# An unconditional fast arm, two more unsplit heads, a new spread of weight conversions, and first loads in three pieces

## The chip, the cores and the metric

One core of one Trainium2 chip runs the program. The metric is device time in microseconds of one execution; the median of several executions is compared. One more execution was taken with the hardware profiler; its trace counts time from the first instruction of the program (its span).

## The reference, cut to what matters

Inputs are float32 apart from the two counts. The weights of the two mixing blocks come as float64 and are converted on the chip.

```python
# attention: B, H, S, D = 2, 8, 768, 64; n_global, n_local = 8, 96
scores = (q @ k^T) / sqrt(D)
keep = (column < n_global) or (0 <= row - column < n_local)
dist = n_local where global and not local, else |row - column|
scores = where(keep, scores - 2**-(h + 1) * dist, -1e9)
a = softmax(scores);  x = a @ v, as (B, S, 512)
# first mixing block
theta = x @ w_theta
y = w_tok_r @ (x * cos(theta)) + w_tok_i @ (x * sin(theta))
u = x + y;  x = u + relu(u @ w_ch)
# second mixing block, d_ff = 1024
h = relu(x @ w_in);  c = convolution of 3 taps of h along the sequence
out = (h * sigmoid(c)) @ w_out
```

The counts n_global and n_local are read on the chip. With at most 8 global columns and 1 to 97 local ones a row of 128 queries needs only a band of keys.

## The kernel before, in words

There are two arms. `run_fast` computes the banded attention and then the mixing blocks; `run_general` computes full rows of scores for any counts, and the same mixing blocks. `begin` runs ahead of both: it issues the first loads, keeps TensorE occupied with four products of zeros (`idle`), reads the two counts (`words`, `nf`), makes the table of distances and masks (`table`), and makes `fi`, which is 1 if the counts fit the band. Then line 1023 loads `fi` from SBUF into a register of each engine, and the branch of line 1026 picks the arm. The general arm lies behind the fast one in every engine's program, so an engine that has finished the fast arm jumps over it.

In the fast arm one head is 768 queries in six tiles of 128, handled in three steps of two tiles. The loop variable `j` counts these steps, `i, tp = divmod(j, 3)`, with 16 heads `i`, so j runs to NJ = 48 and on until the pipeline is empty. In each step the order on every engine is written out by hand: scores of step j (TensorE, into PSUM), softmax of j-1 (VectorE adds the table and takes the row minimum, `L378`), exponentials of j-2 or so (ScalarE, `L387`), transposes, copies to SBUF, products with v, and after three steps the division by the row sums (`L296` to `L298`).

Scores are made in two ways. Heads in `WHOLE` (0 to 7) multiply float32 by float32 as loaded: one product per tile, which the trace shows as two instructions. Other heads are split: ScalarE makes a rounded copy of the scaled queries (`L306`), VectorE makes the remainder of queries (`L310`) and of keys (`L92`, `qk<-a`, 64x816), and each tile takes two products of rounded operands. The rounded keys of a split head come by a DMA of GpSimd that converts (`keys`), but for head 10 (`ROUND`), where ScalarE makes them. Whole heads come in pairs of one load of keys and two of queries (`pair`), into parts of `scratch` and of the output tile of the second batch.

Beside the heads the loop runs the weight conveyor (`Net.run(k)` takes k steps). A weight tile takes six steps, four of them one VectorE instruction each (`L104`, `L108`, `L112` on `wbit`, and the remainder, `L92`, `wt<-wbit`), two of them one ScalarE instruction each. Twelve tiles (72 steps) are done in the attention, the other 36 in `Mix.tail`. After every pair of heads the finished output is transposed (`X<-ident,xs`), and from head 11 on `theta_0` adds six products of `theta` to each step. When the heads are through, `theta1` and `Mix.tail` do the rest: token mixing, channel mixing, `ff_in` with its gate, and `ff_out`, which writes the result.

```python
        if i > 0 and i + 1 not in WHOLE:
            if tp == 0:
                att.split(i + 1, "A A" if i + 1 in ROUND else "  A")
...
        if 7 < j <= NJ:
            net.run((3, 2, 3)[tp] if i > 10 else 2 if i < 7 else 1)
```

Of the kernel before, what the change touches and what calls it, by code (L numbers as in the profile page):

```python
# [12 lines left out]
F32 = mybir.dt.float32  # L13
F32R = mybir.dt.float32r
I32 = mybir.dt.int32
AF = mybir.ActivationFunctionType
ALU = mybir.AluOpType
# [4 lines left out]
P = 128  # L22
# [17 lines left out]
TWO_PI = 2.0 * math.pi  # L40
TURN = 6.283185
TWO32 = float(2.0 ** 32)
WHOLE = range(8)
ROUND = (10,)
LAG_SM, LAG_EXP, LAG_T, LAG_EV, LAG_PV, LAG_N = 1, 2, 3, 4, 5, 6


# [179 lines left out]
class Attention:  # L227
# [21 lines left out]
    def load(self, i, whole=False):  # L249
        if whole or (i < NH and i not in WHOLE):  # L250
            b, h = divmod(i, H)
            src, st = self.net.io["qk"][b, :, h, :], self.st[i % 2]
            if whole or i in ROUND:
                self.nc.sync.dma_start(st, src)
            else:
                self.nc.sync.dma_start(st[:, 0:S], src[:, 0:S])
                self.nc.sync.dma_start(st[D:P, S:STAGE], src[D:P, S:STAGE])

    def keys(self, i):
        if i < NH and i not in WHOLE and i not in ROUND:  # L260
            b, h = divmod(i, H)
            self.nc.gpsimd.dma_start(self.K(i), self.net.io["qk"][b, :, h, S:STAGE])

# [202 lines left out]
class Mix:  # L466
# [237 lines left out]
    def tail(self, early):  # L704
# [151 lines left out]
            n.run(4)  # L856
        pipe.drain()
        n.finish(48)
        for b in range(2):
            for t in range(NT):  # L860
                halves = [slice(0, DM // 2), slice(DM // 2, DM)] if (b, t) == (1, NT - 1) else [slice(0, DM)]
                for c in halves:
                    self.ff_out(b, t, bank(), "V" if c.start or t % 2 == 0 else "A", c)


def run_fast(tc, net):
# [2 lines left out]
    att = FastAttention(net, xs)  # L869
    mix = Mix(net, xs)  # L870
    nc.scalar.activation(att.whole[3][0:D], net.head["half_pi"][0:D].to_broadcast([D, S]), AF.Copy, scale=0.0)
    att.tables(1)
    nc.gpsimd.memset(att.whole[2][D:P], 0.0)
    att.load_v(0)
    att.pair(2)
    att.load_v(1)
# [31 lines left out]
    for j in range(NJ + LAG_N + 3):  # L908
# [23 lines left out]
                att.keys(i + 2)  # L932
        if i > 0 and i + 1 not in WHOLE:
            if tp == 0:
                att.split(i + 1, "A A" if i + 1 in ROUND else "  A")
            elif tp == 1:
                att.split(i + 1, "   V")
                att.split(i + 1, " V")
# [26 lines left out]
            next(early, None)  # L965
        if j == 4:
            net.fetch()
        if 7 < j <= NJ:
            net.run((3, 2, 3)[tp] if i > 10 else 2 if i < 7 else 1)
    last.drain()  # L970
    mix.tail(early)


# [36 lines left out]
def arm(tc, io, head, run):  # L1010
    with tc.tile_pool(name="small", bufs=1) as small, tc.tile_pool(name="slots", bufs=1) as slots, tc.tile_pool(
        name="ps", bufs=1, space=bass.MemoryType.PSUM
    ) as ps, tc.manual_schedule():
        run(tc, Net(tc, io, small, slots, ps, head))


def build(nc, io):
    with tile.TileContext(nc) as tc, tc.tile_pool(name="const", bufs=1) as small:
        head = {}
        net = Net(tc, io, small, None, None, head)  # L1020
        with tc.tile_pool(name="idle", bufs=1, space=bass.MemoryType.PSUM) as ps, tc.manual_schedule():
            begin(nc, io, net, small, head, ps.tile([P, 512], F32, name="idle"))
        rv = nc.values_load(
            head["flag"][:1, :1], min_val=0, max_val=1, skip_runtime_bounds_check_because="it is the product of comparisons, 0 or 1"
        )
        with tc.If(rv == 1) as cmp:
            arm(tc, io, head, run_fast)
        with cmp.Else():
            arm(tc, io, head, run_general)


def begin(nc, io, net, small, head, idle):
# [1 line left out]
    w = small.tile([P, 4], I32, name="words")  # L1034
    scratch = small.tile([P, 2584], F32, name="scratch")
    nc.scalar.dma_start(w, io["n"].bitcast(I32).rearrange("(o n) -> o n", o=1).to_broadcast([P, 4]))
    for x in (slice(0, 2 * KW), slice(2 * KW, NT * KW)):
        nc.sync.dma_start(scratch[:, S:STAGE][:, x], io["pairs"][0, :, x])
    nc.sync.dma_start(scratch[D:P, STAGE : STAGE + S], io["qk"][0, D:P, 1, 0:S])
    qc = (slice(0, 2 * P), slice(2 * P, S))  # L1040
    for x in qc:
        nc.scalar.dma_start(scratch[0:D, x], io["qk"][0, 0:D, 0, x])
    nc.vector.memset(scratch[D:P, 0:S], 0.0)
    zero = nc.const_aps.tensor(0.0, [P, 512], F32)
    for x in (512, 512, 512, 128):
        net.mm(idle[:, 0:x], zero[:, 0:P], zero[:, 0:x], True, True)
    nc.vector.memset(scratch[0:D, STAGE : STAGE + S], 0.0)

# [18 lines left out]
    nc.vector.scalar_tensor_tensor(f[:, 4:6], lo2, 0.0, hi2, op0=ALU.is_lt, op1=ALU.add)  # L1067
    nc.vector.scalar_tensor_tensor(f[:, 6:8], f[:, 4:6], TWO32, lo2, op0=ALU.mult, op1=ALU.add)
    ng, nl = f[:, 6:7], f[:, 7:8]
    flag = small.tile([1, 2], F32, name="flag")  # L1070
    fi = small.tile([1, 1], I32, name="fi")
    nc.vector.tensor_scalar(flag[:, 0:1], nl[0:1], 1.0, None, op0=ALU.is_ge)
    nc.vector.scalar_tensor_tensor(flag[:, 1:2], nl[0:1], float(NPREV + 1), flag[:, 0:1], op0=ALU.is_le, op1=ALU.mult)
    nc.vector.scalar_tensor_tensor(fi, ng[0:1], float(NG), flag[:, 1:2], op0=ALU.is_le, op1=ALU.mult)
    far = small.tile([P, NG], F32, name="far")
    nc.gpsimd.tensor_scalar(far, R[:, G], ng, BIG, op0=ALU.is_ge, op1=ALU.mult)
    nc.gpsimd.tensor_scalar(far, far, nl, FIRST, op0=ALU.max, op1=ALU.mult)
# [3 lines left out]
    nc.vector.tensor_tensor(X[:, 0:NG], X[:, 0:NG], far, op=ALU.max)  # L1081
    nc.vector.tensor_copy(T[:, G], far)
    nnl = small.tile([P, 1], F32, name="nnl")
    head.update(scratch=scratch, qk0=qk0, table=table, ident=ident, half_pi=hp[:, 0:1], ng=ng, nl=nl, nnl=nnl, flag=fi)


# [34 lines left out]
```

## Time and profile before

| what | value |
| --- | --- |
| median of 3 runs | 409.94 us (407.86 to 410.41) |
| profiled execution, its own time | 407.4 us |
| its span, first to last instruction | 405.5 us |
| TensorE matmuls (PE) busy | 398.0 us, 98% |
| weight loads (PEld) busy | 375.5 us, 93% |
| VectorE (DVE) busy | 323.5 us, 80% |
| ScalarE (ACT) busy | 222.2 us, 55% |
| GpSimd (POOL) busy | 27.0 us, 7% |

The profiled execution's own time is 1.9 us longer than its span and 2.5 us shorter than the median. Busy shares are means over stages with different limits: from 134.4 us to the end TensorE alone is full, while in the attention TensorE and VectorE are both nearly full. A busy PE is a row of pipelined matmuls with modelled ends, so a full PE may still be slower than it could be.

### The profile page before, as it was taken

Reading aid. Unit: us, or ns where it says so; the run is one execution under the profiler, and the core shown is the slowest. Engines: PE = TensorE matmul, PEld = TensorE weight load, DVE = VectorE, ACT = ScalarE, POOL = GpSimd, SP = SyncE. Lnnn points to the kernel's source line nnn. Section 1 sums busy time; section 2 is a strip of 40 time slices with the busy share of each in tenths; the row PEclk is TensorE's granted clock in tenths of the full one; section 3 lists DMA queues with packets and bytes.
Section 4 is the critical chain, followed back from the end, with each engine's and each line's share of the span. In section 5 each row is a group of like instructions: output and inputs, shape, how many; then the busy total and the mean of one; then the engine's idle time right before and its main releaser. Section 6 shows DMA issues by size and latency. Waiting matters only on the chain.

```text
span 405.5 us, 6477 instructions
## 1 busy us (share of the span) xinstructions
PE 398.0 (98%) x2384; PEld 375.5 (93%) x2384; DVE 323.5 (80%) x712; ACT 222.2 (55%) x436; POOL 27.0 (7%) x35
## 2 busy tenths in 40 slices
PE   8999998999999999999999999999999999999995
PEld 5999997899998999999999999999999998888885
DVE  5679999999668869999899999998999999700001
ACT  4888989778777877335353336455654454200000
POOL 5214133111000000000000000000000000000000
PEclk9999999999999999999999999999999999999999
DMA  6968968773100231246464332130000000210111
GB/s 158 326 186 254 291 190 244 232 218 83 34 2 0 81 116 39 79 126 189 154 208 158 135 125 103 54 105 2 0 2 0 2 0 2 78 52 29 51 52 60
DMA packets 15575, 42.73 MB, mean 105 GB/s; under 512 B 2096, under 2 KB 2544, under 8 KB 15536
## 3 DMA queue, kind: packets, MB, share of 16 engines
q1 hardware_dynamic: 13936, 38.87, 30.7%
q0 software_dynamic: 1008, 2.92, 2.5%
q10 hardware_dynamic: 592, 0.46, 0.4%
q8 instruction: 20, 0.33, 0.3%
q14 instruction: 19, 0.16, 0.1%
HBM read 39.10 MB, written 3.15 MB: 104 GB/s over the span
## 4 chain that ended last, share of the span: by engine, by line
PE 89%; DVE 7%; DMA 1%; issue 1%; ACT 1%; DVEq 0%
PE O L95 24%; PE S L95 22%; PE PT L95 16%; PE TH L95 14%; PE X L95 9%; PE PT L396 3%; DVE a L378 2%; DVE qk L92 1%; DVE qk L310 1%; DMA words<-n 1%; PE X L520 1%; DVE xTs L92 1%; DVE xTs L88 0%; DVE wbit L112 0%; DVE wbit L108 0%
## 5 line engine op out<-in xcount | busy, mean ns | idle before, releaser
L387 ACT ACTIVATE a<-a,nm 128x232 f32<-128x232 f32 (+1 forms) x96 | 40.1, 471 | 8.4 <-DVE nm L378 8.1
L95 PE MATMUL O<-a,a 128*128 128x65 f32 x236 | 29.9, 268 | 0.0
L378 DVE CUSTOM_DVE_ANT_0 a<-S,qk 128x232 f32<-128x232 f32 (+1 forms) x72 | 23.9, 370 | 7.2 <-PE PT L396 5.7
L95 PEld LDWEIGHTS O<-a,a 128*128 128x128 f32 x236 | 29.0, 192 | 0.2
L84 ACT ACTIVATE a<-PT 128x512 f32<-128x512 f32 (+1 forms) x48 | 26.5, 553 | 4.2 <-PE PT L396 4.2
L100 ACT ACTIVATE wbit<-wst 128x512 f32<-128x512 f32 (+1 forms) x38 | 23.3, 616 | 9.6 <-DMA wst<-w_ch 2.9
L396 PE MATMUL PT<-ident,a 128*128 128x128 f32 x176 | 27.1, 273 | 0.0
L95 PE MATMUL O<-wt,z 128*128 128x384 f32 x144 | 26.9, 334 | 0.0
L95 PE MATMUL TH<-wth,xTs 128*128 128x512 f32 x96 | 26.2, 408 | 0.4 <-ACT scratch L564 0.4
L95 PE MATMUL PT<-wt,z 128*128 128x384 f32 x132 | 25.8, 334 | 0.0
L112 DVE SCALAR_TENSOR_TENSOR wbit<-wst,wbit 128x512 int32<-128x512 int32 (+1 forms) x38 | 24.6, 647 | 1.0
L95 PEld LDWEIGHTS O<-wt,z 128*128 128x128 f32 x144 | 25.2, 188 | 0.1
L108 DVE SCALAR_TENSOR_TENSOR wbit<-wst,wbit 128x512 int32<-128x512 int32 (+1 forms) x38 | 24.0, 632 | 0.9
L84 ACT ACTIVATE wt<-wbit 128x384 fp32r<-128x384 f32 x24 | 12.6, 526 | 21.9 <-DVE wbit L112 12.3
L104 DVE TENSOR_SCALAR wbit<-wbit 128x512 int32<-128x512 int32 (+1 forms) x48 | 18.9, 394 | 5.4 <-ACT wbit L100 5.3
L342 POOL TENSOR_SCALAR qk<-table 128x360 fp32r<-128x360 f32 x15 | 19.9, 1326 | 50.1 <-DVE nm L378 49.0
L95 PEld LDWEIGHTS PT<-wt,z 128*128 128x128 f32 x132 | 23.1, 188 | 0.0
L396 PEld LDWEIGHTS PT<-ident,a 128*128 128x128 f32 x176 | 20.8, 141 | 1.3
L95 PE MATMUL S<-wt,z 128*128 128x384 f32 x120 | 22.0, 335 | 0.0
L95 PEld LDWEIGHTS S<-wt,z 128*128 128x128 f32 x120 | 20.9, 188 | 0.0
L95 PEld LDWEIGHTS TH<-wth,xTs 128*128 128x128 f32 x96 | 17.0, 189 | 3.8 <-ACT scratch L564 0.7
L95 PE MATMUL O<-x,win 128*128 128x384 f32 x96 | 17.4, 336 | 0.0
(218 smaller groups left out, 942.6 us busy)
## 6 DMA issues: line engine op xcount, KB each, us to landing
wst<-w_tok SPq DMA_DIRECT2D x18, 384.0 KB, 3.4
a<-v SPq DMA_DIRECT2D x16, 357.5 KB, 5.7
wst<-w_out SPq DMA_DIRECT2D x8, 512.0 KB, 3.2
qk<-qk POOLq DMA_DIRECT2D x7, 408.0 KB, 5.7
out<-scratch SPq DMA_DIRECT2D x11, 256.0 KB, 2.0
a<-qk SPq DMA_DIRECT2D x7, 384.0 KB, 4.7
wst<-w_in SPq DMA_DIRECT2D x5, 512.0 KB, 3.3
scratch<-w_tok SPq DMA_DIRECT2D x6, 384.0 KB, 3.3
```

The source lines that it names most:

```text
L84: self.nc.scalar.activation(out, in_, AF.Copy)
L92: e.tensor_tensor(out, in_, hi.bitcast(F32), op=ALU.subtract)
L95: self.nc.tensor.matmul(out, l, r, start=start, stop=stop)
L100: self.nc.scalar.activation(t.bitcast(F32), w[:, 1 : w.shape[1] : 2].bitcast(F32), AF.Copy, scale=REBIAS)
L104: self.nc.vector.tensor_scalar(t, t, 3, None, op0=ALU.logical_shift_left)
L108: self.nc.vector.scalar_tensor_tensor(t, w[:, 0 : w.shape[1] : 2], 29, t, op0=ALU.logical_shift_right, op1=ALU.bitwise_or)
L112: self.nc.vector.scalar_tensor_tensor(t, w[:, 1 : w.shape[1] : 2], -(1 << 31), t, op0=ALU.bitwise_and, op1=ALU.bitwise_or)
L310: nc.vector.scalar_tensor_tensor(lo, q, QSCALE, hi.bitcast(F32), op0=ALU.mult, op1=ALU.subtract)
L342: self.nc.gpsimd.tensor_scalar(self.bias[i % 2], self.net.head["table"], x / FIRST, None, op0=ALU.mult)
L378: self.nc.vector.tensor_tensor_reduce(self.sS[tp][:, c], s["sp"][:, c], t, scale=QSCALE if i in WHOLE else 1.0, scalar=3.0e38, op0=ALU.add ...
L387: self.nc.scalar.activation(sS[:, c], sS[:, c], AF.Exp, bias=s["nm"][:, u : u + 1], scale=-1.0)
L396: self.nc.tensor.transpose(pt[:, c], sS[:, self.columns(u, a)], net.head["ident"])
```

## The change: what it does

- The branch at the start is gone. The fast arm runs in any case; the three VectorE instructions that make the flag move into `fits`, called behind the heads' loop. The flag's load into registers (`choose`) is called before `ff_out`, and behind the fast arm the general arm follows under a condition, flag = 0. It then overwrites the output.
- `WHOLE` takes in heads 8 and 9, and `ROUND` is dropped, so head 10 gets its rounded keys by GpSimd's DMA.
- The conveyor's steps are spread anew. Before: 2 in step 8, 6 a head in heads 3 to 6, 3 a head in 7 to 10, 8 a head from 11 on. After: 4 in head 2, 5 a head in 3 to 9, none in head 10, 6 a head in 11 to 15, and one a step behind the heads until nothing is left.
- First loads: the keys of the first pair come in three pieces of 272 columns on ScalarE's queue, the queries of head 0 in three pieces of 256 on SyncE's; before, two pieces each, on the other queue. One of the four products of zeros is dropped.
- GpSimd clears half of one tile before it makes the table of head 1, not after.

```diff
--- before.py
+++ after.py
@@ -40,8 +40,7 @@
 TWO_PI = 2.0 * math.pi
 TURN = 6.283185
 TWO32 = float(2.0 ** 32)
-WHOLE = range(8)
-ROUND = (10,)
+WHOLE = range(10)
 LAG_SM, LAG_EXP, LAG_T, LAG_EV, LAG_PV, LAG_N = 1, 2, 3, 4, 5, 6
 
 
@@ -250,14 +249,14 @@
         if whole or (i < NH and i not in WHOLE):
             b, h = divmod(i, H)
             src, st = self.net.io["qk"][b, :, h, :], self.st[i % 2]
-            if whole or i in ROUND:
+            if whole:
                 self.nc.sync.dma_start(st, src)
             else:
                 self.nc.sync.dma_start(st[:, 0:S], src[:, 0:S])
                 self.nc.sync.dma_start(st[D:P, S:STAGE], src[D:P, S:STAGE])
 
     def keys(self, i):
-        if i < NH and i not in WHOLE and i not in ROUND:
+        if i < NH and i not in WHOLE:
             b, h = divmod(i, H)
             self.nc.gpsimd.dma_start(self.K(i), self.net.io["qk"][b, :, h, S:STAGE])
 
@@ -856,6 +855,7 @@
             n.run(4)
         pipe.drain()
         n.finish(48)
+        n.head.get("choose", lambda: None)()
         for b in range(2):
             for t in range(NT):
                 halves = [slice(0, DM // 2), slice(DM // 2, DM)] if (b, t) == (1, NT - 1) else [slice(0, DM)]
@@ -869,8 +869,8 @@
     att = FastAttention(net, xs)
     mix = Mix(net, xs)
     nc.scalar.activation(att.whole[3][0:D], net.head["half_pi"][0:D].to_broadcast([D, S]), AF.Copy, scale=0.0)
+    nc.gpsimd.memset(att.whole[2][D:P], 0.0)
     att.tables(1)
-    nc.gpsimd.memset(att.whole[2][D:P], 0.0)
     att.load_v(0)
     att.pair(2)
     att.load_v(1)
@@ -932,7 +932,7 @@
                 att.keys(i + 2)
         if i > 0 and i + 1 not in WHOLE:
             if tp == 0:
-                att.split(i + 1, "A A" if i + 1 in ROUND else "  A")
+                att.split(i + 1, "  A")
             elif tp == 1:
                 att.split(i + 1, "   V")
                 att.split(i + 1, " V")
@@ -965,9 +965,10 @@
             next(early, None)
         if j == 4:
             net.fetch()
-        if 7 < j <= NJ:
-            net.run((3, 2, 3)[tp] if i > 10 else 2 if i < 7 else 1)
+        if 6 < j < NJ + 9 and i != 10:
+            net.run(1 if j >= NJ or 2 < i < 10 and tp == 2 else 2)
     last.drain()
+    fits(nc, net.head)
     mix.tail(early)
 
 
@@ -1020,12 +1021,15 @@
         net = Net(tc, io, small, None, None, head)
         with tc.tile_pool(name="idle", bufs=1, space=bass.MemoryType.PSUM) as ps, tc.manual_schedule():
             begin(nc, io, net, small, head, ps.tile([P, 512], F32, name="idle"))
-        rv = nc.values_load(
-            head["flag"][:1, :1], min_val=0, max_val=1, skip_runtime_bounds_check_because="it is the product of comparisons, 0 or 1"
-        )
-        with tc.If(rv == 1) as cmp:
-            arm(tc, io, head, run_fast)
-        with cmp.Else():
+        def choose():
+            head["rv"] = nc.values_load(
+                head["flag"][:1, :1], min_val=0, max_val=1, skip_runtime_bounds_check_because="it is the product of comparisons, 0 or 1"
+            )
+
+        head["choose"] = choose
+        arm(tc, io, head, run_fast)
+        del head["choose"]
+        with tc.If(head["rv"] == 0, preferred_fallthrough_block=False):
             arm(tc, io, head, run_general)
 
 
@@ -1034,15 +1038,14 @@
     w = small.tile([P, 4], I32, name="words")
     scratch = small.tile([P, 2584], F32, name="scratch")
     nc.scalar.dma_start(w, io["n"].bitcast(I32).rearrange("(o n) -> o n", o=1).to_broadcast([P, 4]))
-    for x in (slice(0, 2 * KW), slice(2 * KW, NT * KW)):
-        nc.sync.dma_start(scratch[:, S:STAGE][:, x], io["pairs"][0, :, x])
+    for x in range(0, NT, 2):
+        k, q = slice(x * KW, x * KW + 2 * KW), slice(x * P, x * P + 2 * P)
+        nc.scalar.dma_start(scratch[:, S:STAGE][:, k], io["pairs"][0, :, k])
+        nc.sync.dma_start(scratch[0:D, q], io["qk"][0, 0:D, 0, q])
     nc.sync.dma_start(scratch[D:P, STAGE : STAGE + S], io["qk"][0, D:P, 1, 0:S])
-    qc = (slice(0, 2 * P), slice(2 * P, S))
-    for x in qc:
-        nc.scalar.dma_start(scratch[0:D, x], io["qk"][0, 0:D, 0, x])
     nc.vector.memset(scratch[D:P, 0:S], 0.0)
     zero = nc.const_aps.tensor(0.0, [P, 512], F32)
-    for x in (512, 512, 512, 128):
+    for x in (512, 512, 128):
         net.mm(idle[:, 0:x], zero[:, 0:P], zero[:, 0:x], True, True)
     nc.vector.memset(scratch[0:D, STAGE : STAGE + S], 0.0)
 
@@ -1067,11 +1070,6 @@
     nc.vector.scalar_tensor_tensor(f[:, 4:6], lo2, 0.0, hi2, op0=ALU.is_lt, op1=ALU.add)
     nc.vector.scalar_tensor_tensor(f[:, 6:8], f[:, 4:6], TWO32, lo2, op0=ALU.mult, op1=ALU.add)
     ng, nl = f[:, 6:7], f[:, 7:8]
-    flag = small.tile([1, 2], F32, name="flag")
-    fi = small.tile([1, 1], I32, name="fi")
-    nc.vector.tensor_scalar(flag[:, 0:1], nl[0:1], 1.0, None, op0=ALU.is_ge)
-    nc.vector.scalar_tensor_tensor(flag[:, 1:2], nl[0:1], float(NPREV + 1), flag[:, 0:1], op0=ALU.is_le, op1=ALU.mult)
-    nc.vector.scalar_tensor_tensor(fi, ng[0:1], float(NG), flag[:, 1:2], op0=ALU.is_le, op1=ALU.mult)
     far = small.tile([P, NG], F32, name="far")
     nc.gpsimd.tensor_scalar(far, R[:, G], ng, BIG, op0=ALU.is_ge, op1=ALU.mult)
     nc.gpsimd.tensor_scalar(far, far, nl, FIRST, op0=ALU.max, op1=ALU.mult)
@@ -1081,7 +1079,15 @@
     nc.vector.tensor_tensor(X[:, 0:NG], X[:, 0:NG], far, op=ALU.max)
     nc.vector.tensor_copy(T[:, G], far)
     nnl = small.tile([P, 1], F32, name="nnl")
-    head.update(scratch=scratch, qk0=qk0, table=table, ident=ident, half_pi=hp[:, 0:1], ng=ng, nl=nl, nnl=nnl, flag=fi)
+    head["part"], head["flag"] = small.tile([1, 2], F32, name="part"), small.tile([1, 1], I32, name="flag")
+    head.update(scratch=scratch, qk0=qk0, table=table, ident=ident, half_pi=hp[:, 0:1], ng=ng, nl=nl, nnl=nnl)
+
+
+def fits(nc, head):
+    ng, nl, flag, fi = (head[x] for x in ("ng", "nl", "part", "flag"))
+    nc.vector.tensor_scalar(flag[:, 0:1], nl[0:1], 1.0, None, op0=ALU.is_ge)
+    nc.vector.scalar_tensor_tensor(flag[:, 1:2], nl[0:1], float(NPREV + 1), flag[:, 0:1], op0=ALU.is_le, op1=ALU.mult)
+    nc.vector.scalar_tensor_tensor(fi, ng[0:1], float(NG), flag[:, 1:2], op0=ALU.is_le, op1=ALU.mult)
 
 
 def kernel(q, k, v, n_global, n_local, moe_w_theta, moe_w_tok_r, moe_w_tok_i, moe_w_ch, moe2_w_in, moe2_conv_w, moe2_w_out):
```

## Rows read from the trace of the kernel before

**Rows 1.** One head each: us, busy us of PE, PEld, DVE, ACT, POOL; clock, DMA.

```profile
36.67:43.08 6.41, 6.41 (x53) 6.20 (x53) 6.27 (x22) 5.30 (x14) 2.21 (x2) 1.00 0.77 234
43.08:48.90 5.82, 5.82 (x47) 5.62 (x47) 5.69 (x20) 5.01 (x13) 1.27 (x1) 1.00 0.94 289
48.90:54.46 5.56, 5.56 (x53) 5.56 (x53) 5.50 (x17) 4.88 (x12) 1.68 (x1) 1.00 0.65 217
54.46:59.60 5.14, 5.14 (x47) 5.08 (x46) 5.01 (x18) 5.14 (x12) 1.86 (x2) 1.00 0.80 223
85.89:95.09 9.20, 9.20 (x64) 8.38 (x63) 8.97 (x28) 7.46 (x16) 1.77 (x3) 1.00 0.63 183
95.09:104.86 9.77, 9.77 (x71) 8.94 (x70) 8.01 (x24) 7.97 (x19) 1.18 (x1) 1.00 0.24 73
```

**Rows 2.** The same view, heads 10 to 12 in one stretch.

```profile
59.60:85.89 26.29, 24.36 (x179) 22.19 (x178) 25.57 (x81) 21.09 (x49) 5.76 (x6) 1.00 0.82 229
```

**Rows 3.** VectorE in order of time at the start: start us, us, what.

```profile
4.94 0.14 DVE L1072 TENSOR_SCALAR flag<-nf 1x1 f32<-1x1 f32 x1
...
6.61 0.16 DVE L1082 COPY table<-far 128x8 f32<-128x8 f32 x1
7.46 0.29 DVE L378 CUSTOM_DVE_ANT_0 a<-S,table 128x128 f32<-128x128 f32 x1 [0.69 <-PE S L95]
```

**Rows 4.** The flag's load on line 1023: duration ns, then first and last start.

```profile
L1023 DVEq TENSOR_LOAD <-fi x1: 541/541/541, 6.6 to 6.6; - x1
```

**Rows 5.** The chain that ended last, first 14 us: start, us, what.

```profile
6.46 1.64 PE S L95 x8
8.09 0.78 PE TH L95 x4
```

**Rows 6.** ScalarE's queue in order of time, its loads of queries.

```profile
1.18 1.17 ACTq L1042 DMA_DIRECT2D scratch<-qk  x2
```

**Rows 7.** DMA issues of the first 14 us: KB each, us to landing.

```profile
scratch<-pairs SPq DMA_DIRECT2D x1, 136.0 KB, 3.6
...
scratch<-qk ACTq DMA_DIRECT2D x1, 64.0 KB, 4.5
```

**Rows 8.** Groups by form, first 6.3 us: busy us, mean ns, idle before.

```profile
L95 PE MATMUL idle<-const-float32-0.0 128*128 128x512 f32 x6 | 5.2, 1040 | 0.8 <-PEq L1114 0.8
```

**Rows 9.** Groups by form, 43.08 to 104.86 us.

```profile
L92 DVE TENSOR_TENSOR qk<-a,qk 64x816 fp32r<-64x816 f32 x8 | 8.0, 1006 | 0.2
L310 DVE SCALAR_TENSOR_TENSOR qk<-a,qk 128x768 fp32r<-128x768 f32 x8 | 7.6, 953 | 0.0
...
L112 DVE SCALAR_TENSOR_TENSOR wbit<-wst,wbit 128x384 int32<-128x384 int32 x8 | 4.7, 592 | 0.1
...
L92 DVE TENSOR_TENSOR wt<-wbit,wt 128x384 fp32r<-128x384 f32 x7 | 4.2, 593 | 0.1
...
L104 DVE TENSOR_SCALAR wbit<-wbit 128x384 int32<-128x384 int32 x7 | 2.8, 402 | 0.3 <-ACT wbit L100 0.2
```

**Rows 10.** In order of time behind the heads: VectorE, and the product that needs it.

```profile
113.91 0.96 DVE L92 TENSOR_TENSOR xTs<-xT,xTs 128x768 fp32r<-128x768 f32 x1
...
115.34 1.64 PE L95 MATMUL TH<-wth,xTs 128*128 128x512 f32 x6
```

**Rows 11.** VectorE in order of time, last idle stretch before the token mixing.

```profile
120.15 0.17 DVE L296 TENSOR_SCALAR rs<-O 128x6 f32<-128x6 f32 x1 [2.93 <-PE O L95]
```

**Rows 12.** The branches of line 1026: duration ns, first and last start.

```profile
L1026 ACTq COMPARE_BRANCH  x2: 38/43/48, 6.0 to 401.9; - x2
...
L1026 PEldq COMPARE_BRANCH  x2: 90/1690/3290, 6.1 to 398.7; - x2
```

**Rows 13.** The chain that ended last, from 395 us.

```profile
398.07 2.89 PE S L95 x24
```

**Rows 14.** What follows the branch (line 1018): duration ns, first and last start.

```profile
L1018 SPq DRAIN  x3: 7/7/13, 403.9 to 405.0; - x3
...
L1018 ACTq DRAIN  x2: 8/44/80, 404.6 to 405.0; - x2
```

## Prediction

> **What bounds the kernel now.** I read the stretches of one head each first, then the start in order of time, then the end. Behind 134 us TensorE alone is full, and the change touches that part only with a register load and at its very end. In the attention two engines are nearly full at once. Heads 6 and 7, whole, took 6.41 and 5.82 us with PE busy throughout; heads 8 and 9, split, took 5.56 and 5.14, PE again busy throughout, and DVE busy 10.51 of their 10.70 [rows 1]. Heads 13 and 14, with theta beside them, took 9.20 and 9.77, PE full [rows 1]. Between them lie heads 10 to 12: 26.29 us, DVE busy 25.57 of them, PE 24.36 [rows 2]. That is the one long stretch where VectorE sets the pace, and so the one where taking work off VectorE can pay; in the others it is PE's work that counts. PE's busy time flatters it: a full PE can still be late where the modelled ends hide a gap, so I also compare heads of like work.
>
> **The change part by part.**
>
> **Start.** The first softmax begins at 7.46, though the table is ready at 6.77 [rows 3]: between them VectorE loads the flag (0.54, from 6.6) and branches [rows 4]. PE, which needs no table, starts its first scores at 6.46 [rows 5], behind the same load and branch on its own queue. The change takes away both, and the three flag instructions ahead of the table. The first of these starts at 4.94 [rows 3] and each holds VectorE about as long as its 0.14 to 0.17 and a gap, together 0.45. The table is then ready at 6.77 - 0.45 = 6.32, and with the scores there the first softmax starts at about 6.35: 1.1 us earlier. Are the scores there? They need the first piece of keys and of queries. Before, the queries' piece was issued on ScalarE's queue at 1.18 [rows 6] and took 4.5 us, landing at 5.7; the keys' piece, first on SyncE's, took 3.6 [rows 7]. The queues are exchanged, so now the keys are second on ScalarE's queue, from 1.18: landing between 1.18 + 3.6 = 4.8 and 5.7 or so. Scores of step 0 take 0.6 us (1.64 for eight instructions [rows 5], two thirds of the columns of the second four): done between 5.4 and 6.3, at the slow clock level by 6.5. I take 1.0 us of gain, bounds 0.8 and 1.1. The later steps need the second and third pieces; the other transfers of the arm (values, next pair), which stood behind the branch on SyncE's queue, are issued at about 3 us and share the DMA engines with them, but each step of scores after the first takes 0.78 [rows 5], so a piece may come 0.8 us after the one before and no one waits.
>
> A rule of the Trainium skill speaks against this part. "DMA: Bandwidth & Descriptors", in its section on queues, rings and completion order, says that each DMA engine takes turns between the queues it has work for, a packet from one and then one from the next. By it the keys, 408 KB alone on ScalarE's queue, get half of the engines as soon as SyncE's queue holds a backlog, and the third piece lands last of the first loads; what step 2 then waited would come off the 1.0; no row here shows such a share, and a landing in the trace after the change can.
>
> The fourth product of zeros that goes is two of the eight instructions; six of 128x512 took 5.2 us [rows 8], so PE falls idle some 1.7 us earlier, from 6.2 to about 4.5, and stays idle until the keys land: 0.3 to 1.2 us. Cost by itself nothing, since the scores could not start; what it may do to the clock is a rival below. GpSimd's clearing ahead of the table of head 1 costs nothing: that table is wanted three steps later.
>
> **Heads 8 and 9 whole.** PE pays. A whole head with the transposes of the output took 6.41, a split one with them 5.56; without them 5.82 and 5.14 [rows 1]. So 0.85 + 0.68 = 1.5 us more, all on the path, as PE was full in both kinds. VectorE saves per head one remainder of queries, 0.95, and one of keys, 1.01 [rows 9]: 3.9 us. ScalarE saves its copies too, and that of head 10's keys; it was nowhere full. Loads: three on SyncE's queue (one of keys, two of queries) for the pair in place of four, and two conversions by GpSimd's DMA fewer, one for head 10 more, issued three heads ahead into a buffer that nobody then reads. No cost.
>
> **Conversions.** A tile of 384 columns costs VectorE 0.40 + 0.59 + 0.59 + 0.59 = 2.2 us (the instruction of line 108 taken as that of 112) in six steps [rows 9]: 0.36 a step. Heads 7 to 9 take 15 steps, not 9: +2.2 us, against the 3.9 saved, so VectorE has 1.7 us less in them while PE takes 1.5 more. It is then ahead, not behind, when head 10 begins. Heads 10 to 12 take 0 + 6 + 6 = 12 steps, not 3 + 8 + 8 = 19: -2.5 us, which leaves VectorE 25.57 - 2.5 = 23.1. What would PE need there? Head 10, with transposes and no theta, as head 8: 5.56. Head 12, with transposes and theta in three steps, as head 14: 9.77. Head 11, with theta in two steps: 9.20 less a third of the difference of heads 13 and 9, (9.20 - 5.14) / 3 = 1.35, so 7.85. Together 23.2 against 26.29. The gain is then 3.1 if PE never waits; PE's visible idle time alone is 26.29 - 24.36 = 1.9 [rows 2]; and if only VectorE's uneven load (a head without theta holds the same softmax as one with it, in less time) is what counts, perhaps 1.0. Both engines would need 23.1 to 23.2, and two full engines seldom fit without a gap; VectorE's head start speaks for more than 1.9. I take 2.6, bounds 1.0 and 3.1.
>
> Behind, the conveyor has more to do: head 15 takes 6 steps, not 2, which VectorE's slack there hides, and steps 48 to 50 take one each, two of them the last remainders, 0.59 each. They fall just where VectorE splits the output for the next stage: that ends at 114.87, and PE needs it for the product at 115.34 [rows 10]. Slack 0.47 against 0.59 to 1.2: cost 0.1 to 0.7, below nothing excluded since nothing is taken away there. I take 0.3. The flag instructions, 0.45, come later, in front of the first token mixing, where VectorE had 2.9 idle just before [rows 11] and its results wait several us for PE: nothing. If that cover were gone they would cost their 0.45.
>
> **Tail.** The flag's load on PE's queue ahead of `ff_out` would stop PE for half a microsecond [rows 4] if PE's sequencer did not run ahead. It does: its last branch starts at 398.7 [rows 12], while the last products run until 398.07 + 2.89 = 400.96 [rows 13], 2.3 us ahead. So nothing, bound +0.5. Nobody else is wanted there. At the end each engine jumps over the general arm, and the jump is dear: ScalarE's branch stands at 401.9 and its next instruction only at 404.6 [rows 12, 14]; on PE the branch alone took 3.29. SyncE, which jumped early and waits for the last landing, is through at 403.9 [rows 14], so ScalarE's jump sets the end, by 0.65. If the skipped arm is laid out behind the end, nobody jumps, and that 0.65 goes. Bounds 0 and -0.65.
>
> **Sum.** -1.0 + 1.5 - 2.6 + 0.3 - 0.65 = -2.45. The profiled execution, 407.4 (a span of 405.5), would come to 405.0. The median of the runs shown lies 2.5 above it for a reason that the trace doesn't show; I take the sum off the median: 407.5 us. With every bound the good way: -1.1 + 1.5 - 3.1 + 0.1 - 0.65 = -3.25. The bad way: -0.8 + 1.5 - 1.0 + 0.7 + 0.5 = +0.9.
>
> **The rivals.**
>
> *VectorE still sets the pace in heads 10 to 12.* Then the gain there is 1.0, and PE's added 1.5 stays: 409.94 - 0.85 = 409.1. For it: VectorE was busy 97% there, and softmax of a head without theta is as long as with it. Against: 2.5 us leave that stretch, and head 10 loses all its steps.
>
> *The clock comes late: slower.* Six instructions of 512 columns in 5.2 us are 1.7 ns a column [rows 8]; four of 232 columns in 0.78 us are 0.84 [rows 5]. So the engine ran at 1.2 GHz during the products of zeros and at 2.4 soon after, having worked without a break from 0.8 us. With one product of zeros less it idles 0.3 to 1.2 us between them and the scores. Should that break put the rise off to 10.5, say, PE's work until then runs at half speed; PE is on the path from 6.46 on, so of 4 to 4.5 us half is lost, 2.2, and if the ramp's own gaps put it off to 13, 3.5. The time would be 409.7 to 411.0; I take 411.0. It decides once the rise comes later than about 11. Against: the gap may be short, and the ramp is partly held by the chain of softmax.
>
> *The skip is still a jump.* Then the end stays: 409.94 - 1.8 = 408.1. The Trainium skill, "Runtime: NRT & Kernel Launch", section on instruction fetch, says that a taken branch to code outside the window already fetched waits for that code to be fetched; the trace agrees, with 3.29 us on PE. By it everything hangs on the layout, which the diff asks for but no row can show.
>
> **How the numbers follow.** Chances: the forecast 0.57; VectorE's pace 0.15; the jump 0.12; the clock 0.11; more gain than the bounds sum up, from gaps hidden in PE's busy time, 0.05 (405.5). The likeliest gives 407.5. The range reaches from below the best sum, 406.7, by a microsecond for the runs' own spread (2.5 us from lowest to highest), to the middle of the slow case: 405.5 to 410.8. About 1% is what a measurement of this kernel can tell from no change: 405.8 to 414.0. Below it falls part of the best case and of the runs' spread, 0.14; above it almost nothing, 0.03; within 0.83.
>
> **What would show it.** First softmax at 6.3 to 6.6. PE busy throughout head 10, heads 8 and 9 at 6.4 and 5.8, heads 10 to 12 in 23 to 24.5. The first of the products with `xTs` behind the heads idle 0.1 to 0.7 before it. No gap on PE ahead of `ff_out`. ScalarE's last drain right behind its branch, the end within 1.5 us of the last landing. Wrong it would be by a clock that rises later than 6 us, by a wait of PE in heads 8 to 12 that VectorE or GpSimd's DMA ends, or by synchronisation of the arms at the condition.

## The result, and the profile after

The changed kernel took 411.97 us (median of 9 runs, 411.01 to 412.88), the kernel before 407.96 beside it (9 runs, 406.95 to 410.45). The ratio is 1.0085, with a 95% interval of 1.0059 to 1.0111: slower by 0.6 to 1.1%. The profiled execution took 412.46 us, with a span of 410.7 against 405.5.

TensorE did as much as before, so the added time is idle time or work of others. The page's first part, of the changed kernel (engine, busy us, share, instructions):

```profile
PE 398.6 (97%) x2382; PEld 375.8 (92%) x2382; DVE 319.5 (78%) x708; ACT 220.2 (54%) x433; POOL 26.6 (6%) x34
```

**The start.** The table's work now begins as soon as the words are there, without flag, load or branch. VectorE in order of time, changed kernel (the rows that answer to [rows 3]):

```profile
3.86 0.34 DVE L1076 TENSOR_SCALAR table<-scratch,nf 128x232 f32<-128x232 f32 x1
...
5.10 0.16 DVE L1080 COPY table<-far 128x8 f32<-128x8 f32 x1
5.92 0.29 DVE L377 CUSTOM_DVE_ANT_0 a<-S,table 128x128 f32<-128x128 f32 x1 [0.65 <-PE S L94]
```

The first softmax came at 5.92 in place of 7.46, 1.54 us earlier. Head 1 began only 0.50 earlier (8.21 against 8.71), and this is what was kept to head 8. TensorE in order of time shows where the other microsecond went, and the second view, line 1043 alone, why (its middle line: who waited for it, us and times; the last line: us from issue to landing of its three pieces of keys):

```profile
5.00 1.67 PE L94 MATMUL S<-scratch 128*128 128x128 f32 x8
7.35 1.02 PE L94 MATMUL TH<-scratch 128*128 128x232 f32 x4 [0.69 <-DMA scratch<-pairs]
8.21 0.78 PE L94 MATMUL S<-scratch 128*128 128x128 f32 x4
```

```profile
L1043 ACTq DMA_DIRECT2D scratch<-pairs x3: 450/453/581, 1.1 to 2.1; - x3
...
  PE TH L94: 0.7, 1
...
DMA to landing us min/median/max: 3.0/3.2/5.1
```

The scores began at 5.00 [rows 5: 6.46] and the third step then waited 0.69 for the third piece of keys: issued at 2.10, it took 5.1 us and landed at 7.22, where the first took 3.0 (the first of before took 3.6 [rows 7]).

**Heads 8 to 12.** One head or stretch a row, changed kernel, columns as in [rows 1]:

```profile
48.43:54.84 6.41, 6.41 (x54) 6.20 (x53) 5.64 (x21) 5.14 (x13) 2.21 (x2) 1.00 1.12 328
54.84:60.66 5.82, 5.82 (x48) 5.61 (x47) 5.13 (x19) 4.97 (x13) 1.10 (x1) 1.00 0.68 209
60.66:85.54 24.88, 23.94 (x180) 21.82 (x179) 23.31 (x72) 19.46 (x44) 6.80 (x7) 1.00 0.80 208
```

Heads 8 and 9 cost 12.23 us in place of 10.70 [rows 1], +1.53. Heads 10 to 12 took 24.88 in place of 26.29 [rows 2], -1.41: VectorE's work there fell by 2.26, TensorE's idle time by 0.99 to 0.94. Heads 13 and 14 did not change (9.19 and 9.77 [rows 1]).

**Behind the heads.** From head 15's first scores to the first product of the token mixing the changed kernel took 30.75 us, the one before 29.80: +0.95. VectorE in order of time, changed kernel:

```profile
110.86 0.55 DVE L107 SCALAR_TENSOR_TENSOR wbit<-wst,wbit 128x384 int32<-128x384 int32 x1
111.44 0.56 DVE L111 SCALAR_TENSOR_TENSOR wbit<-wst,wbit 128x384 int32<-128x384 int32 x1
111.92 0.69 DVE L565 SCALAR_TENSOR_TENSOR r<-scratch,r 128x512 f32<-128x512 f32 x1
112.52 0.39 DVE L377 CUSTOM_DVE_ANT_0 a<-S,qk 128x232 f32<-128x232 f32 x1
...
114.50 0.55 DVE L91 TENSOR_TENSOR wt<-wbit,wt 128x384 fp32r<-128x384 f32 x1
114.97 0.95 DVE L91 TENSOR_TENSOR xTs<-xT,xTs 128x768 fp32r<-128x768 f32 x1
```

The last softmax, at 111.8 before, starts at 112.52 behind two conveyor steps, though the heads ran 0.36 us earlier; these two are the last of head 15's six (j = 47). And the split of `xTs` that began at 113.91 [rows 10] began at 114.97 behind a third, the first of those behind the heads. From the first token product to the last product of the program both took 266.29: the flag's load ahead of `ff_out` cost nothing.

**The end.** From the last product to the end the kernel before needed 4.58 us, the changed one 9.12: +4.55, most of the loss. Lines 1032 (the condition) and 1019 (what follows it), changed kernel: duration ns, first and last start.

```profile
L1032 SPq EVENT_SEMAPHORE  x8: 17/17/17, 397.1 to 405.4; - x8
...
L1032 SPq COMPARE_BRANCH  x2: 43/46/49, 397.0 to 405.5; - x2
L1032 PEldq COMPARE_BRANCH  x2: 83/1920/3757, 399.2 to 401.7; - x2
```

```profile
L1019 SPq EVENT_SEMAPHORE  x13: 17/28/28, 409.1 to 410.6; - x13
...
L1019 SPq DRAIN  x3: 7/7/13, 409.8 to 410.1; - x3
...
L1019 ACTq DRAIN  x2: 8/44/80, 405.8 to 410.1; - x2
```

SyncE reaches the condition at 397.0, waits there for the last landing (eight semaphore instructions, the last at 405.4), branches a second time at 405.5, and its next instruction stands at 409.1: 3.6 us in which no engine has anything to do. ScalarE was through at 405.8. Before, SyncE branched at 396.4 while TensorE still worked, and was drained at 403.9 [rows 14]; its branches of line 1026, kernel before:

```profile
L1026 SPq COMPARE_BRANCH  x2: 43/46/49, 6.0 to 396.4; - x2
```

The landing that SyncE waits for came late as well: the last transfer took 3.2 us (402.09 to 405.26), before 2.1. By the trace's records of single DMA packets, fifteen of its sixteen shares had landed by 404.17. The sixteenth began at 404.03, just as a packet of 16 KB ended (402.69 to 404.04) that belongs to a queue of instructions (changed kernel, 401 to 406 us: packets, MB, share of 16 engines):

```profile
q10 hardware_dynamic: 144, 0.13, 8.4%
q8 instruction: 1, 0.02, 1.7%
```

Before, such a packet (399.58 to 400.58) held up a share of the transfer before the last in the same way, beside TensorE's last products, where nobody waited for it. In both traces the packet starts 0.9 to 1.0 us after TensorE's last branch, which the change moved from 398.7, ahead of the last product's end, to 401.7, behind it.

The parts add up to the difference of the spans: -0.50 + 1.53 - 1.41 + 0.95 + 4.55 = +5.1. Each is read from one execution. Over the profiles of all kernels below that share the part, heads 8 and 9 whole (12.22 to 12.24 us) and the stretch behind the heads (30.74 to 30.77 with the new spread, 29.80 to 29.82 with the old) hardly vary; the start with these first loads gained 0.48 to 0.91, heads 10 to 12 with heads 8 and 9 whole and the new spread took 24.10 to 24.88, and the tail with this layout and the long arm 8.3 to 9.2. The medians differ by 4.0: the profiled run before was among its faster ones (407.4 of 406.95 to 410.45), the one after among its slower; runs of the kernel before at 409.7 us and more, where two of the three behind the prediction's 409.94 lie, show a mean granted clock of 0.99 wherever a clock is on record, and its others 0.997 or more.

### The profile page after: what moved, and what is told of

It is laid out like the page before. It is cut to its first block, busy times and chain, and to the rows that moved or that the text cites. A ratio compares the mean times of both kernels' runs of the same rounds, so it can differ in the third digit from the quotient of the medians.

```text
span 410.7 us, 6481 instructions
## 1 busy us (share of the span) xinstructions
PE 398.6 (97%) x2382; PEld 375.8 (92%) x2382; DVE 319.5 (78%) x708; ACT 220.2 (54%) x433; POOL 26.6 (6%) x34
## 6 DMA issues: line engine op xcount, KB each, us to landing
a<-v SPq DMA_DIRECT2D x16, 357.5 KB, 5.4
```

## The experiments

Theory: SyncE waits for the output at the end of the arm and only then jumps over the general arm; that jump takes as long as PE's did [rows 12] and lies bare at the end. First rival: the end is late for what was added ahead of it (flag, load, other spread). Second: the whole heads and the new spread cost the time in the attention. Unless said otherwise the edit is made to the changed kernel.

**The other layout.**

```diff
-        with tc.If(head["rv"] == 0, preferred_fallthrough_block=False):
+        with tc.If(head["rv"] == 0, preferred_fallthrough_block=True):
```

> The changed kernel with the general arm preferred as the block that follows the branch, so that whoever skips it jumps at the condition itself. Main theory: SyncE waits at the condition for the last output to land and only then jumps, 3.6 us, with nothing beside it; now it jumps at about 397, while TensorE still works, and the end comes about 1 us behind the last landing: span 407 to 407.5 (410.7 after), time 408 to 409. Rival, the synchronisation at the condition costs the time and not the jump: the end stays some 5 us behind the last landing, time 411.5 to 412.5.

Measured: 407.82 us, ratio to the kernel before 1.0003 (0.9992 to 1.0015). Line 1032 of this kernel:

```profile
L1032 SPq EVENT_SEMAPHORE  x8: 17/17/17, 399.5 to 404.0; - x8
...
L1032 SPq COMPARE_BRANCH  x1: 45/45/45, 396.6 to 396.6; - x1
L1032 PEldq COMPARE_BRANCH  x1: 3837/3837/3837, 398.8 to 398.8; - x1
```

SyncE's jump now comes first, from 396.6 to 399.5, beside TensorE's last products, and the waits stand behind it. The tail is 4.66 us; one word took 4.15 us off the time. That is 0.2 more than expected: TensorE's branch stands at 398.8, ahead of the last product's end again, and the last transfer took 2.1 us and landed at 403.80.

**The branch back at the start**, the rest as changed: `choose` and the condition go, `fits` is called in `begin`, and the two arms stand under If and Else.

```diff
-        arm(tc, io, head, run_fast)
...
-        with tc.If(head["rv"] == 0, preferred_fallthrough_block=False):
+        with tc.If(rv == 1) as cmp:
+            arm(tc, io, head, run_fast)
+        with cmp.Else():
             arm(tc, io, head, run_general)
```

> The changed kernel with the branch back at the start (flag made there, general arm as the other branch), all else as changed. Main theory: the tail falls from 9.1 us behind the last product to about 4.6, the start gives back what the missing branch gained (0.5 to 1.5), so 408 to 409.3. Rival, the attention itself is what got slower by its heads and conversions: the time stays above 411.

Measured: 407.21 us, 0.9986 (0.9969 to 1.0003). The tail is 4.36; the first softmax comes at 6.91, a microsecond after the changed kernel's, and yet head 1 begins at 7.84, before the changed kernel's 8.21. An earlier softmax was not what the start needed. The time is 0.8 under what was expected.

**Heads 8 and 9 split again**, with the new spread.

```diff
-WHOLE = range(10)
+WHOLE = range(8)
+ROUND = (10,)
...
-                att.split(i + 1, "  A")
+                att.split(i + 1, "A A" if i + 1 in ROUND else "  A")
```

> The changed kernel with heads 8 and 9 split and head 10's keys rounded by ScalarE again, the new spread kept. By PE's price: heads 8 and 9 take 1.5 us less; VectorE gets 3.9 us more work ahead of head 10, so heads 10 to 12 take 1 to 2 us more. If PE's price and VectorE's relief are equal, 411.5 to 412.5; if VectorE is the scarcer engine, 412.5 to 413.5; if PE's price is never earned back, 410.3 to 411.3.

Measured: 414.81 us, 1.0176 (1.0154 to 1.0199), 2.8 over the changed kernel: more than any of the three cases gave. Heads 8 to 11 of this kernel, columns as in [rows 1]:

```profile
48.06:53.69 5.63, 5.63 (x54) 5.62 (x53) 5.53 (x16) 5.05 (x12) 1.68 (x1) 1.00 0.70 252
53.69:61.16 7.47, 5.61 (x48) 5.16 (x46) 7.20 (x23) 5.99 (x13) 1.69 (x2) 1.00 0.72 204
61.16:68.34 7.18, 7.18 (x54) 7.18 (x53) 7.01 (x26) 5.78 (x15) 1.99 (x2) 0.76 0.84 246
68.34:77.88 9.54, 8.30 (x59) 7.07 (x59) 6.91 (x21) 5.17 (x13) 2.10 (x3) 1.00 0.80 226
```

In head 9 VectorE is busy 7.20 of 7.47 us and TensorE 5.61; the granted clock then fell to 1.2 GHz from 61.87 to 65.28, and products of head 10 ran at half speed. The four heads took 29.82 us, in the changed kernel 26.43. The loss does not hang on the clock: one of the five runs has a mean granted clock of 0.994, as the changed kernel's runs have (0.991 to 0.995), and took 414.81 us all the same. VectorE, busy for 14.21 of the 14.65 us of heads 9 and 10, is the likelier cause: the spread of five steps a head needs the whole heads.

**The old spread**, the rest as changed.

```diff
-        if 6 < j < NJ + 9 and i != 10:
-            net.run(1 if j >= NJ or 2 < i < 10 and tp == 2 else 2)
+        if 7 < j <= NJ:
+            net.run((3, 2, 3)[tp] if i > 10 else 2 if i < 7 else 1)
```

> The changed kernel with the conveyor's steps spread as before. If the steps in head 15 and behind the heads cost what the trace shows there (1.0 us, products waiting for the transposed output), that comes back; 8 steps a head in 11 and 12 for 6, and 3 in head 10 for none, cost up to 1.5 us there. Sum -1.0 to +0.6: 411.0 to 412.6. If the rest of the loss is the spread's, below 410.5.

Measured: 410.81 us, 1.0078 (1.0058 to 1.0098), 1.16 under the changed kernel. Heads 10 to 12, and head 15 with what follows:

```profile
60.86:85.68 24.82, 24.09 (x179) 21.79 (x179) 23.48 (x73) 19.75 (x46) 5.78 (x6) 1.00 0.75 203
104.64:134.46 29.82, 29.82 (x186) 26.22 (x184) 22.77 (x53) 23.45 (x45) 0.00 (x0) 1.00 0.01 2
```

The time lies between the two cases expected. The 0.95 behind the heads goes, with `fits` still in its place, so the conveyor's late steps, in head 15 and behind the heads, are its cause. Heads 10 to 12 are as short here as with the new spread. One execution of each does not settle what the steps taken out of them gain: in the profiles with heads 8 and 9 whole these heads took 24.10 to 24.88 us with the new spread (four) and 24.45 to 25.76 with the old (seven), some half microsecond less on average, and less than the 0.95.

**Both remedies together**: the other layout and the old spread.

> The changed kernel with the skipped arm laid out as the way on (preferred_fallthrough_block True) and with the conveyor line of before. If the two costs are separate, they add: 411.97 - 4.15 - 1.16 = 406.7 us; tail behind the last product 4.6, head 15 to the first token product 29.8. If the old spread only pays while the end is late, about 407.8, as with True alone.

Measured: 406.54 us, 0.9956 (0.9940 to 0.9973); tail 4.53, head 15 and behind 29.82. The two costs are separate and add.

**The queues of the first loads exchanged**, on top of that.

```diff
-        nc.scalar.dma_start(scratch[:, S:STAGE][:, k], io["pairs"][0, :, k])
-        nc.sync.dma_start(scratch[0:D, q], io["qk"][0, 0:D, 0, q])
+        nc.sync.dma_start(scratch[:, S:STAGE][:, k], io["pairs"][0, :, k])
+        nc.scalar.dma_start(scratch[0:D, q], io["qk"][0, 0:D, 0, q])
```

> As e5_true_old, with the queues of the first loads swapped: the three key pieces on SyncE's queue, ahead of the arm's bulk loads there, the query pieces on ScalarE's. If the third key piece is late (7.22 us) because it shares the transfers with the bulk loads of the other queue, it now lands near 6.2, TensorE's wait of 0.7 us at 7.35 goes, and the time is 0.4 to 0.7 under e5_true_old, about 406.1. If the bytes ahead of it set its time on any queue, it lands near 7.2 again and the time is that of e5_true_old; if the query piece takes over the lateness on ScalarE's queue, the same.

Measured: 406.49 us, 0.9951 (0.9930 to 0.9972), no more than e5_true_old. Line 1043 of this kernel, and TensorE in order of time:

```profile
L1043 SPq DMA_DIRECT2D scratch<-pairs x3: 392/417/424, 0.7 to 1.6; - x3
...
DMA to landing us min/median/max: 3.0/3.2/3.4
```

```profile
5.00 2.32 PE L94 MATMUL S<-scratch 128*128 128x128 f32 x8
7.16 0.95 PE L94 MATMUL TH<-scratch 128*128 128x232 f32 x4
7.95 0.78 PE L94 MATMUL S<-scratch 128*128 128x128 f32 x4
```

The third piece takes 3.4 us in place of 5.1 and TensorE waits for no load: the queues and their order set its time. The arm's bulk loads, which the expectation blamed, are not needed for the delay: in e2_branch_first, where SyncE issues them from 4.93 on and not from 3.38, the piece landed at 6.85, and in six profiles with these first loads and the bulk loads ahead between 6.60 and 7.24. What is left in the other queue are the loads of queries. The time did not follow, as far as six and eight runs can tell. In the profiled execution TensorE ran at 1.2 GHz until 6.38, where the trace's clock record begins (products of 0.59 us); the changed kernel's clock had risen at 4.81, and the eight instructions took 2.32 us here and 1.67 there. The rule from the Trainium skill quoted in the prediction, that engines take turns between queues ("DMA: Bandwidth & Descriptors", queues, rings and completion order), agrees with the landings of the third piece, 3.4 us and 5.1 us after its issue.

**Whole heads alone**: the kernel before with `WHOLE = range(10)` and `ROUND` dropped, nothing else.

> The kernel before with heads 8 and 9 unsplit and nothing else changed. By the prediction's terms +1.5 in heads 8 and 9 and -2.6 in heads 10 to 12: 407.7 - 1.1 = 406.6 us. By what the changed kernel and its version with the old spread showed, heads 10 to 12 give 1.4 to 1.5 back: 407.7, no change.

Measured: 407.52 us, 0.9989 (0.9974 to 1.0003). Heads 8, 9, and 10 to 12 of this kernel:

```profile
48.83:55.24 6.41, 6.41 (x54) 6.20 (x53) 4.70 (x21) 5.14 (x13) 2.37 (x2) 1.00 1.16 292
55.24:61.06 5.82, 5.82 (x48) 5.61 (x47) 5.27 (x18) 5.02 (x12) 1.27 (x1) 1.00 0.80 226
61.06:85.79 24.73, 24.02 (x180) 21.79 (x179) 23.48 (x73) 19.75 (x46) 5.78 (x6) 1.00 0.76 210
```

TensorE pays 1.53 and gets 1.56 back: an exchange at par. That heads 10 to 12 give about 1.5 and not 2.6 is what the second expectation said.

**The branch alone**: the kernel before with the branch moved behind the arm as in the change, the flag still made at the start.

> The kernel before with only the branch moved behind the arm (general arm under flag = 0, not preferred as the way on); the flag is still made at the start. If SyncE's wait and then its jump are the cost, the tail is 8 to 9 us and not 4.6; with 0.4 to 0.6 saved at the start the time is 411.2 to 411.7 us. If the late end came from the other parts of the change, about 407.2.

Measured: 412.97 us, 1.0111 (1.0094 to 1.0128). Its condition and what follows on SyncE:

```profile
L1032 SPq COMPARE_BRANCH  x2: 43/46/49, 399.2 to 407.8; - x2
...
L1032 PEldq COMPARE_BRANCH  x2: 83/1880/3677, 401.4 to 403.9; - x2
```

```profile
L1019 SPq EVENT_SEMAPHORE  x14: 17/28/28, 411.3 to 412.8; - x14
```

The tail is 9.17 us, 4.59 more than before, and SyncE's 3.5 us from 407.8 to 411.3 are there without any other part of the change. At the start the first softmax came 0.59 earlier, head 1 only 0.09. The time is 1.3 over what was expected, the tail 0.2. (In the profiled execution, 414.7 us, the granted clock was 1.2 GHz from 69.8 to 76.7 us.)

**The general arm cut short.** To tell the layout from the length: the arm under the condition holds seven instructions (the general attention and its mixing are left out; these inputs skip them).

```diff
+def run_short(tc, net):
+    nc = net.nc
+    t = net.slot("xs0", [P, NT, DM], F32, "xs")
+    nc.vector.memset(t[:, 0], 0.0)
+    nc.gpsimd.memset(t[:, 1], 0.0)
+    nc.scalar.activation(t[:, 2], t[:, 0], AF.Copy, scale=1.0)
...
-            arm(tc, io, head, run_general)
+            arm(tc, io, head, run_short)
```

> The changed kernel, with the general arm under the condition cut to seven instructions (two memsets, a copy, a product, a copy, a load within SBUF; the general attention and its mixing are left out, which these inputs skip anyway). If SyncE's 3.6 us after its last branch are the fetch of instructions from behind a long arm, they go: tail 4.4 to 5.6 and not 9.1, time 407.2 to 408.5 us. If any branch taken at the end costs it, whatever it skips, the tail stays at 9 and the time at 412.

Measured: 408.15 us, 1.0008 (0.9995 to 1.0021), tail 5.08. Its condition, and the drains behind it:

```profile
L1044 SPq COMPARE_BRANCH  x2: 38/46/53, 396.2 to 396.4; - x2
L1044 PEldq COMPARE_BRANCH  x2: 83/196/310, 398.5 to 400.9; - x2
```

```profile
L1031 SPq EVENT_SEMAPHORE  x13: 17/28/1234, 396.6 to 405.8; - x13
...
L1031 SPq DRAIN  x3: 7/7/118, 404.9 to 405.5; - x3
```

SyncE goes on 0.2 us behind its branch, and TensorE's branch takes 310 ns in place of 3757. So what a jump costs is set by the length of the code jumped over. This agrees with the Trainium skill, "Runtime: NRT & Kernel Launch", its section on instruction fetch, as the prediction quoted it. The short tail itself has two causes that this run does not part: the order changed too, as line 1044 has a single semaphore instruction on SyncE (396.3) where line 1032 had eight, and the wait for the last landing (404.74) stands behind the jump here as with the other layout.

**Fewer and more products of zeros**, on the kernel e6_keys_on_sync (512, 512, 128 columns there): two, then four.

```diff
-    for x in (512, 512, 128):
+    for x in (512, 512):
```

> As e6_keys_on_sync, with two products of zeros at the start in place of three. In e6 the row of zeros ends at 4.96 us and the scores begin at 5.00 with their operands there at 4.65. If the end of the row holds the scores, they begin at about 4.65 and the time is 0.2 to 0.3 under e6, about 406.2 us. If the shorter row lets the clock rise later, the products stay at 0.59 us each for longer and the time is that of e6 or up to 0.5 over it.

```diff
-    for x in (512, 512, 128):
+    for x in (512, 512, 512, 128):
```

> As e6_keys_on_sync, with the fourth product of zeros of the kernel before put back. If the end of the row holds the scores, they begin at 5.9 to 6.4 us, with the clock up by then, head 1 begins 0.3 to 0.7 later than in e6 (7.95) and the time is 406.8 to 407.2 us. If the longer row pays by an earlier clock, no later than e6: 406.5.

Measured: 406.30 us with two, 0.9955 (0.9938 to 0.9971), and 407.19 with four, 0.9976 (0.9958 to 0.9994). With two the scores began at 4.75 and head 1 at 7.46, with three at 5.00 and 7.95, with four at 6.71 and 8.99: the row of zeros does hold the scores. Two are no better than three beyond what the runs can tell; in the profiled execution (407.23 us) the half microsecond, and 0.8 more, was lost in head 11 (9.51 us, with three products 8.20), to this wait of VectorE (waits of 60 to 80 us: total, times, longest):

```profile
DVE qk L91 <- DMA qk<-qk: 1.7, 1, 1.7
...
PE TH L94 <- DVE xTs L91: 0.8, 1, 0.8
```

The rounded keys of head 12 are issued by GpSimd at 64.90 and land at 71.99. The changed kernel waited 1.1 us in the same place, the kernel before never: VectorE came to them later.

**The load of v later**, to take its 357.5 KB away from beside those keys, on e9_two_products.

```diff
-        if i > 0 and tp == 2 and i + 1 < NH:
-            att.load_v(i + 1)
+        if 1 < i < NH and tp == 0:
+            att.load_v(i)
```

> As e9_two_products, with each head's load of v (357.5 KB) issued one step of two tiles later. In e9 VectorE waits 1.7 us at 70.3 us for the rounded keys of head 12, issued by GpSimd at 64.90 and landed at 71.99, beside the load of v of head 11 (64.78 to 72.23). If the load of v holds them back, the keys land 1 to 2 us sooner after their issue, the wait goes, head 11 takes 8.2 us as in e6 and not 9.51, and the time is 0.3 to 1.0 under e9, about 405.6 us. If the keys' own transfer or its later start sets it, the wait stays and the time is 406.3.

Measured: 406.45 us, 0.9967 (0.9953 to 0.9980), and nothing is decided: the load of v of head 11 was issued at 64.89 (64.78 in e9). In both kernels it directly follows the same load (64.37 and 64.26) in SyncE's own order, so the edit did not move it; the next load of v, which now stands behind a load of weights, came at 77.27 and not at 73.57. The keys landed at 71.87 and the wait was 1.4 us.

The versions with the other layout and the old spread (e5, e6, e9 and e12, 406.3 to 406.5) beat both kernels, the one before by 0.3 to 0.5%, and cannot be told apart.

## Why the prediction was wrong

**The step that failed is the tail.** It said: "If the skipped arm is laid out behind the end, nobody jumps, and that 0.65 goes. Bounds 0 and -0.65." It measured +4.55. I took the condition for one branch per engine that may or may not jump, and the only rival beside it was that the jump stays as it was. What the runs showed is that every engine still jumps, and that the condition orders SyncE's steps anew: first the wait for the last landing, then the jump, 3.6 us long and bare (e1_fall_true, e8_branch_alone). The cost of a jump was in the rows, 3.29 us on PE and 2.7 on ScalarE [rows 12, 14]; that SyncE's was hidden (branch at 396.4, TensorE's products until 400.96 [rows 13]) was the cover whose loss I did not price, although the text named "synchronisation of the arms at the condition" among what would make it wrong. 3.5 of the 4.55 are the jump less what ScalarE's late drain had cost before. The other 1.1 are the last transfer, which took 3.2 us and not 2.1, behind the packet of instructions that follows TensorE's branch. e11_short_arm bears this out: TensorE's last branch stands at 400.9, the packet runs from 401.93 to 403.54, the last share starts at 403.52, and the transfer takes 3.4 us although the arm is short. No run tests it by itself. Freed of the long jump, the end did come as the term had it: in e11 1.1 us behind the last landing, before 1.9.

**The base was 2 us too high.** The sum was taken off 409.94, the median of three runs; nine give 407.96. Off that the same terms give 405.5, so the account missed by 6.5 us and not by 4.5.

**The start, -1.0, was -0.5** (-0.48 to -0.91 over six profiles with this start). The first softmax came even earlier than forecast (5.92 for 6.35). The step "a piece may come 0.8 us after the one before and no one waits" failed: the third piece came 2.4 us after the second. The Trainium skill's rule spoke against just this, and I left it out of the sum. But even without that wait (e6) head 1 gained only 0.26 more, since in that execution the slow clock then sets the pace; the clock's rise varied from 3.84 to 6.86 us between profiles of kernels that differ little. With one product of zeros less as well (e9), head 1 began 1.25 us before that of the kernel before: the forecast 1.0 was to be had, but not by this change. The rival of a late clock, with its rise behind 11 us, did not come about.

**Heads 8 and 9, +1.5, measured +1.53**: right, by comparing heads of like work.

**Heads 10 to 12, -2.6, measured -1.4** (to -2.2 in the other profiles of the new spread), within the bounds. The choice inside them was wrong: the stretch held 1.93 us of idle TensorE, a nearer guide than VectorE's balance, and I went past it for gaps that a modelled end might hide. Of the 1.93, 0.99 were got back; the other 0.42 is less busy time. What remains is theta's wait for ScalarE in head 12 (0.6 us) and 0.3 for a softmax of VectorE, which now waits 1.1 us for the keys of head 12. In e6, TensorE was full in heads 10 and 11 and lost only 0.55 to theta's wait. The rival of VectorE's pace, with a gain of 1.0, came nearer to the size, for the wrong reason.

**Behind the heads, +0.3, measured +0.95**, over its bound of 0.7. I priced the two remainders. Two steps of head 15, which by the prediction "VectorE's slack there hides", pushed the last softmax, and with it exponentials and the transposed output: 0.71 of the 1.06 by which the split of `xTs` came later. They were not in the term.

Without the tail the parts sum to -0.50 + 1.53 - 1.41 + 0.95 = +0.6, and e1_fall_true, the change without the tail's fault, measures no change (its span is 0.3 longer than before, with a start that gained 0.9): the forecast gain of 1.8 outside the tail was not there either.

## What to carry to other kernels

In this kernel every engine pays for a jump over the long block, and the jump is free only while another engine still works. Ask of each engine what it waits for before its jump, and give the block that is nearly never run a layout in which the engine with the last wait jumps first. Where a stretch has a scarce engine, look first at the idle time of the engine on the path (1.93 us here): 2.26 us less work on the scarce one gave 1.41. And work spread away from one crowd must not land in front of the next stage's first operands.

## What was not expected of the hardware

- A branch that skips the general arm held TensorE's queue 3.3 to 3.8 us; one that skips seven instructions 0.31. SyncE's next instruction stood 2.9 to 3.6 us behind such a branch, 0.2 behind the short one.
- One packet of 16 KB on a queue of instructions, 0.9 to 1.0 us behind TensorE's jump, held one of a transfer's sixteen shares back and with it the landing: 3.2 us for 128 KB, and 2.1 where the packet met another transfer.
- The granted clock fell to 1.2 GHz in the attention in two profiles (e3_split_8_9, 61.87 to 65.28; e8_branch_alone, 69.8 to 76.7). In e3 TensorE had just been idle for 1.9 of the 7.47 us of head 9; what sets it stays open.
